# An attention and routing kernel whose engines take their work in the order of the source, with the routed work laid out anew

## The chip, the cores and the metric

The program runs on one core of a Trainium2 chip. The core has a matrix engine (TensorE, PE in the rows; its weight loads are listed apart as PEld), a vector engine (VectorE, DVE), an activation engine (ScalarE, ACT), GpSimd (POOL) and a queue engine that issues transfers (SyncE, SP). Each runs its own list of instructions in order, and semaphores tie the lists together. The metric is the device time of the core in microseconds (us), the median of three runs.

## What is computed

All inputs and outputs are float32.

```python
batch, n_heads, seq, head_dim = (8, 12, 448, 64)
...
scores = scale * np.matmul(q, k.transpose(0, 1, 3, 2)) - np.log(S)
attn = 1.0 / (1.0 + np.exp(-scores))
return np.matmul(attn, v)
...
# bridge: (B,H,S,D) -> (B, S, H*D), D = 768
scores = np.einsum('bsd,d->bs', x, w_gate)
out = x.copy()
for b in range(B):
    top_idx = np.argpartition(-scores[b], capacity)[:capacity]   # capacity 128
    xe = x[b, top_idx]
    h = np.maximum(xe @ w1, 0.0)            # w1: 768 x 1024
    ye = h @ w2                             # w2: 1024 x 768
    g = 1.0 / (1.0 + np.exp(-scores[b, top_idx]))
    out[b, top_idx] = x[b, top_idx] + g[:, None] * ye
```

So each of the 8 images (batch entries) goes through sigmoid attention, and then the 128 of its 448 tokens with the highest gate score go through two dense layers. All others are copied.

## The kernel before

**Attention steps.** The kernel walks through 24 steps `i`, three for each image, each with four heads. `load(i)` has SyncE issue 16 transfers (k, q and two pieces of v). `turn(i)` transposes k and q on VectorE into `kT` and `qT`. `scores(i, n)`, n from 0 to 6, multiplies them on TensorE into a score tile `psc` in PSUM (two buffers), and ScalarE takes its sigmoid into `attnT`; a third group of scores must therefore wait until the sigmoid of the first has read its tile. `values(i)` multiplies `attnT` with v into two tiles `pav`; its first matmuls (line 194) read the last sigmoid's result. VectorE copies `pav` into `xT`. `back(i, pr)`, twice for each step, turns 448 columns of `xT` back with four transposes on TensorE into the PSUM tile `ps`, and VectorE copies that into the image's `x_b`.

**Routed work of an image**, once its `x_b` is whole: `store_and_gate` has SyncE store `x_b` twice (to the output and to a scratch tensor `x_d`) and computes the gate scores on VectorE (four reductions) and a `diag` tile on GpSimd. `rank` has one wide and one small matmul (lines 247, 249), then eight comparisons with sums on VectorE (line 259) and the selection matrix `sel` (line 265). `select` multiplies `sel` with the token numbers (line 274) and has GpSimd gather the chosen rows `xe` from `x_d`. `turn_rows`, two halves, transposes `xe` (line 294). `ffn1` is 8 pieces of six matmuls, with a Relu on ScalarE after each four pieces; `ffn2` is two parts of eight matmuls, each ended by a VectorE instruction into `oe`. `scatter` has GpSimd write `oe` to the output.

**Buffers that bind these together.** `back`, `rank`, `select` and `turn_rows` share one PSUM tile (pool `ps_1`, one buffer; the names `ps_...` in the order rows are its successive uses). `ffn1` and `ffn2` share another (`psf`). `x_b`, `oe`, `sel`, `attnT` and `hT` have one buffer each, so the first copy into the next image's `x_b` must wait until both stores of this image have read it.

**What sets the order.** Each step has two half-steps; a table `places` says which functions belong to half-step `s`, `back` first and the routed work after it. `fill(2*i)` runs between score groups 3 and 4 of step `i`, `fill(2*i + 1)` between group 6 and `values(i)`. That is the order of the source. The framework's scheduler then orders the instructions of each engine anew by priorities and by its own estimates of when inputs are ready, so what an engine runs is not what the source says:

```python
for i in range(NI):
    for n in range(NF + 1):
        scores(i, n)
    if i == 0:
        load_weights()
    fill(2 * i)
...
```

Of the kernel before, what the change touches and what calls it, by code (L numbers as in the profile page):

```python
# [9 lines left out]
F32 = mybir.dt.float32  # L10
# [6 lines left out]
def kernel(  # L17
# [17 lines left out]
    P = 128  # L35
# [3 lines left out]
    NF = 3  # L39
# [4 lines left out]
    KF = F // P  # L44
    ND = D // 2
    NI = B * NQ
# [18 lines left out]
    ps_f = ctx.enter_context(tc.tile_pool(name="ps_f", bufs=1, space=PSUM))  # L65
# [5 lines left out]
    def load(i):  # L71
        b, g = divmod(i, NQ)
        h0 = 4 * g
        tiles = []
        for nm, src in (("k", k), ("q", q)):

            t = raw.tile([P, 2, TB * Dh], F32, name=f"raw_{nm}")
            for j in range(2):
                for e in range(2):
                    p0 = (2 * j + e) * TT  # L80
                    nc.sync.dma_start(  # L81
                        out=t[p0:p0 + TT, :, 0:RUN],
                        in_=bass.AP(
                            tensor=src.tensor,
                            offset=src.offset + (b * H + h0 + j) * S * Dh + e * TT,
                            ap=[[TB * Dh, TT], [2 * S * Dh, 2], [1, RUN]]),
                    )
            tiles.append(t)

        tv = vals.tile([P, 4, NF * Dh], F32, name="raw_v")  # L90
        for m in range(4):
            nc.sync.dma_start(
                out=tv[m * TT:(m + 1) * TT],
                in_=bass.AP(tensor=v.tensor,
                            offset=v.offset + (b * H + h0) * S * Dh + NF * m * Dh,
                            ap=[[TB * Dh, TT], [S * Dh, 4], [1, NF * Dh]]))

        th = vals.tile([P, 2, Dh], F32, name="raw_h")
        for pr in range(2):
            for m in range(2):  # L100
                p0 = (2 * pr + m) * TT
                nc.sync.dma_start(
                    out=th[p0:p0 + TT],
                    in_=bass.AP(tensor=v.tensor,
                                offset=(v.offset + (b * H + h0 + 2 * pr) * S * Dh
                                        + (4 * NF + m) * Dh),
                                ap=[[TB * Dh, TT], [S * Dh, 2], [1, Dh]]))
        raws[i] = tiles + [tv, th]
# [20 lines left out]
    def late_consts():  # L129
        nc.gpsimd.dma_start(  # L130
            out=wg_b,
            in_=bass.AP(tensor=moe_w_gate.tensor, offset=moe_w_gate.offset,
                        ap=[[0, CP]] + [list(x) for x in moe_w_gate.ap]),
        )
        nc.gpsimd.memset(ones, 1.0)
        nc.gpsimd.memset(ones_row, 1.0)
        nc.gpsimd.iota(iota_r, pattern=[[1, CAP]], base=0, channel_multiplier=0,
                       allow_small_or_imprecise_dtypes=True)
        for t in tok_gate:
            nc.gpsimd.iota(t[:, :, 0], pattern=[[CP, NCH]], base=0,  # L140
                           channel_multiplier=1, allow_small_or_imprecise_dtypes=True)
        nc.gpsimd.memset(earlier, 0.0)
        for c in range(NCH):
            nc.gpsimd.affine_select(
                out=earlier[:, c, :], in_=earlier[:, c, :], compare_op=ALU.is_ge,
                fill=1.0, base=-c * CP, pattern=[[1, S]], channel_multiplier=-1)

    def load_weights():
        for w, src in ((w1_sb, moe_w1), (w2_sb, moe_w2)):
            nc.gpsimd.dma_start(out=w, in_=src.rearrange("(t p) f -> p t f", p=P))  # L150
# [4 lines left out]
    def turn(i):  # L155


        kT[i] = head.tile([P, 2, TB, TT], F32, name="kT")
        src = raws[i][0].rearrange("p a (r d) -> p a r d", d=Dh)
        for pr in range(2):  # L160
            nc.vector.transpose(  # L161
                kT[i][:, pr, :4 * NF],
                src[:, pr, :4 * NF, 0:TT].rearrange("p (m c) d -> p c m d", c=NF))
        nc.vector.transpose(kT[i][:, :, 4 * NF:], src[:, :, 4 * NF:, 0:TT])
        qT[i] = head.tile([P, 2, TB, TT], F32, name="qT")
        src = raws[i][1].rearrange("p a (r d) -> p a r d", d=Dh)
        nc.vector.transpose(qT[i], src[:, :, :, 0:TT])  # L167

    def scores(i, n):

        if n == 0:
            attn[i] = attnp.tile([P, 2 * NF + 1, 2, S], F32, name="attnT")
        psc = ps_sc.tile([P, 2, 512], F32, name="psc")
        parts = [(pr, slice(4 * NF, TB), pr * Dh, Dh) for pr in range(2)]
        if n < 2 * NF:
            parts = [(n // NF, slice(4 * (n % NF), 4 * (n % NF) + 4), 0, P)]
        for pr, rows, p0, np_ in parts:
            for j in range(2):
                d = slice(j * Dh, (j + 1) * Dh)
                nc.tensor.matmul(  # L180
                    psc[p0:p0 + np_, j, :S],
                    kT[i][d, pr, rows, :].rearrange("e r t -> e (r t)"),
                    qT[i][d, pr].rearrange("e r t -> e (r t)"),
                    start=True, stop=True)
        nc.scalar.activation(attn[i][:, n], psc[:, :, :S], AF.Sigmoid,  # L185
                             bias=bias_s, scale=QK_SCALE)
# [37 lines left out]
    st = {}  # L224
# [83 lines left out]
        if f % 4 == 3:  # L308
            nc.scalar.activation(st[b]["hT"][:, f - 3:f + 1, :n], ps[:, :, :n], AF.Relu)  # L309

    def ffn2(b, n, part):
        hT = st[b]["hT"]
        if part == 0:
            st[b]["oe"] = moe.tile([P, D], F32, name="oe")
        oe = st[b]["oe"]
        ps = ps_f.tile([P, 512], F32, name="psf")
        cols = slice(part * ND, (part + 1) * ND)
        for t in range(KF):
            nc.tensor.matmul(ps[:n, :ND], hT[:, t, :n], w2_sb[:, t, cols],  # L319
                             start=(t == 0), stop=(t == KF - 1))  # L320
        nc.vector.scalar_tensor_tensor(  # L321
            out=oe[:n, cols], in0=ps[:n, :ND], scalar=st[b]["gate"][:n, 0:1],
            in1=st[b]["xe"][:n, cols], op0=ALU.mult, op1=ALU.add)
# [5 lines left out]
            in_=st[b]["oe"][:n], in_offset=None)  # L329


    places = {}

    def put(s, fn, *args):
        places.setdefault(s, []).append((fn, args))

    def routed(b):
        s = 2 * NQ * (b + 1) + 1
        put(s, store_and_gate, b)
        put(s + 2, rank, b)  # L340
        s += 4
        for s0, n in SLOTS:
            put(s, select, b, s0, n)
            for half in range(2):
                put(s + 1 + half, turn_rows, b, n, half)
            for f in range(KF):
                put(s + 2 + f // 2, ffn1, b, n, f)
            for part in range(2):
                put(s + 2 + KF // 2 + part, ffn2, b, n, part)
            put(s + 2 + KF // 2 + 1, scatter, b, n)  # L350
            s += 2 + KF // 2 + 2

    for i in range(NI):
        put(2 * i + 2, back, i, 0)
        put(2 * i + 3, back, i, 1)
    fills = {s: list(v) for s, v in places.items()}
    places = {}
    for b in range(B):
        routed(b)
    order = {}  # L360
    last = max(places)
    for s in range(last + 1):
        own, rest = fills.get(s, []), places.get(s, [])
        order[s] = own + rest

    def fill(s):
        for fn, args in order.get(s, []):
            fn(*args)

    turn(0)  # L370
    late_consts()
    for i in range(NI):
        for n in range(NF + 1):
            scores(i, n)
        if i == 0:
            load_weights()
        fill(2 * i)
        for n in range(NF + 1, 2 * NF + 1):
            scores(i, n)
        if i + 1 < NI:  # L380
            turn(i + 1)
        if i + 2 < NI:
            load(i + 2)
        fill(2 * i + 1)
        values(i)
    for s in range(2 * NI, last + 1):
        fill(s)


# [27 lines left out]
```

## Time and profile before

| | |
|---|---|
| Time, median of 3 runs | 755.27 us (750.07 to 758.37) |
| The profiled execution's own time | 751.88 us |
| Its span, first to last instruction | 750.1 us |
| TensorE busy with matmuls | 571.5 us (76%) |
| VectorE, ScalarE, GpSimd busy | 229.3, 174.0, 31.2 us |
| Mean granted TensorE clock | 0.899 of full speed |
| DMA, mean over the span | 119 GB/s |

Busy times are sums over the span and say nothing of where an engine stood idle. Each float32 matmul of the program appears as two records in the trace, so a count there is twice that of the order's rows. In the rows, a bracket gives the idle time of the engine just before the first instruction of the row, and who ended it. The difference between time and span, 1.78 us, lies outside the recorded instructions.

### The profile page before, as it was taken

What the parts mean: (1) busy time and instruction counts of PE and PEld (TensorE: products, weight loads), DVE (VectorE), ACT (ScalarE), POOL (GpSimd) and SP (SyncE); (2) the same over time, 40 slices, a digit from 0 to 9 for tenths busy, and PEclk for the clock granted to TensorE, in tenths of its full rate; (3) what the DMA queues carried; (4) which work ended last, traced back from release to release, by engine and by line L of the source; (5) the groups of instructions that cost most, each with busy time, mean ns of one, the idle gap of its engine ahead of it and who ended that gap; (6) DMA issues with size and microseconds to landing.
All of it is one profiled execution on the core that took longest, in us unless ns stands there. A gap on an engine that the chain in (4) does not pass through costs nothing.

```text
span 750.1 us, 7353 instructions
## 1 busy us (share of the span) xinstructions
PE 571.5 (76%) x2896; PEld 295.0 (39%) x2896; DVE 229.3 (31%) x481; ACT 174.0 (23%) x193; POOL 31.2 (4%) x43
## 2 busy tenths in 40 slices
PE   0767678679983889839896599856998388984996
PEld 0222222346332554324542454324633245423873
DVE  1032421642115312254034521164121641225410
ACT  0333243031330322303412033302133033130000
POOL 4000000000000000000000000001000000000010
PEclk9889899869997799959999699987999689995999
DMA  9989595258132673227550392505923251002310
GB/s 247 305 191 207 120 262 124 47 128 237 43 94 69 164 175 77 63 68 205 134 140 1 78 267 64 140 22 116 265 53 94 68 156 64 1 21 61 109 43 21
DMA packets 46995, 88.93 MB, mean 119 GB/s; under 512 B 12848, under 2 KB 25136, under 8 KB 46960
## 3 DMA queue, kind: packets, MB, share of 16 engines
q1 hardware_dynamic: 44288, 75.52, 41.0%
q0 software_dynamic: 2672, 12.93, 5.4%
q8 instruction: 23, 0.38, 0.2%
q14 instruction: 12, 0.10, 0.0%
HBM read 63.26 MB, written 25.17 MB: 118 GB/s over the span
## 4 chain that ended last, share of the span: by engine, by line
PE 58%; DMA 13%; ACT 11%; DVE 10%; issue 6%; SPq 2%; POOLq 0%; DVEq 0%; ACTq 0%
PE pav L200 14%; PE psf L306 12%; PE psc L180 12%; PE psf L319 10%; ACT attnT L185 10%; DMA raw_q<-in_q_dram 5%; DMA xe<-x_d,row 4%; DVE junk L259 3%; PE ps L219 3%; PE pav L194 3%; DMA raw_h<-in_v_dram 2%; PE ps L274 2%; SPq L81 2%; PE ps L294 1%; DVE x_b L221 1%
## 5 line engine op out<-in xcount | busy, mean ns | idle before, releaser
L185 ACT ACTIVATE attnT<-psc,bias_s 128x896 f32<-128x896 f32 x168 | 161.8, 1004 | 292.3 <-PE psc L180 292.0
L180 PE MATMUL psc<-qT,kT 64*128 64x448 f32 (+1 forms) x768 | 165.6, 597 | 48.3 <-DVE qT L167 29.8
L200 PE MATMUL pav<-attnT,raw_v 128*64 128x448 f32 x576 | 124.5, 551 | 0.0
L205 DVE COPY xT<-pav 128x448 f32<-128x448 f32 x48 | 44.2, 923 | 243.1 <-PE pav L200 243.1
L180 PEld LDWEIGHTS psc<-qT,kT 64*128 64x128 f32 (+1 forms) x768 | 53.5, 180 | 151.1 <-ACT attnT L185 101.3
L306 PE MATMUL psf<-xeT,w_sb 128*128 128x128 f32 x768 | 104.6, 297 | 9.4 <-ACT hT L309 4.9
L306 PEld LDWEIGHTS psf<-xeT,w_sb 128*128 128x128 f32 x768 | 99.0, 210 | 18.6 <-DVE xeT L296 7.5
L319 PE MATMUL psf<-w_sb,hT 128*128 128x384 f32 x256 | 90.1, 497 | 10.9 <-ACT hT L309 5.5
L200 PEld LDWEIGHTS pav<-attnT,raw_v 128*64 128x64 f32 x576 | 40.3, 138 | 72.5 <-issue 69.6
L319 PEld LDWEIGHTS psf<-w_sb,hT 128*128 128x128 f32 x256 | 46.3, 189 | 51.7 <-DVE oe L321 9.7
L221 DVE COPY x_b<-ps 112x512 f32<-112x512 f32 x48 | 33.0, 688 | 106.5 <-PE ps L219 105.6
L219 PE MATMUL ps<-iden,xT 128*112 128x128 f32 x192 | 37.8, 329 | 22.7 <-DVE x_b L221 12.0
L274 PE MATMUL ps<-tok_gate,sel 112*128 112x2 f32 x64 | 13.8, 338 | 43.0 <-DVE sel L265 43.0
L219 PEld LDWEIGHTS ps<-iden,xT 128*112 128x112 f32 x192 | 23.5, 154 | 45.9 <-issue 14.8
L194 PE MATMUL pav<-attnT,raw_h 64*64 64x448 f32 x192 | 26.4, 568 | 15.9 <-ACT attnT L185 13.5
L309 ACT ACTIVATE hT<-psf 128x512 f32<-128x512 f32 x16 | 9.6, 597 | 122.6 <-PE psf L306 122.6
L161 DVE STREAM_TRANSPOSE kT<-raw_k 128x384 f32<-128x384 f32 x48 | 25.2, 553 | 34.7 <-DMA raw_k<-in_k_dram 34.7
L281 ACT ACTIVATE gate<-ps 128x1 f32<-128x1 f32 x8 | 1.4, 171 | 143.0 <-DVE idx L279 143.0
L321 DVE SCALAR_TENSOR_TENSOR oe<-psf,gate,xe 128x384 f32<-128x384 f32 x16 | 9.9, 618 | 72.0 <-PE psf L319 70.6
L274 PEld LDWEIGHTS ps<-tok_gate,sel 112*128 112x128 f32 x64 | 13.5, 311 | 45.3 <-issue 45.0
L234 DVE CUSTOM_DVE_ANT_0 junk<-x_b,wg_b 112x768 f32<-112x768 f32 x32 | 30.3, 948 | 1.3
L294 PE MATMUL ps<-iden,xe 128*128 128x128 f32 x48 | 13.1, 407 | 22.9 <-DMA xe<-x_d,row 22.0
(38 smaller groups left out, 171.7 us busy)
## 6 DMA issues: line engine op xcount, KB each, us to landing
raw_k<-in_k_dram SPq DMA_DIRECT2D x96, 216.0 KB, 4.4
raw_q<-in_q_dram SPq DMA_DIRECT2D x96, 216.0 KB, 4.9
out_dram<-x_b SPq DMA_DIRECT2D x8, 1344.0 KB, 6.4
x_d<-x_b SPq DMA_DIRECT2D x8, 1344.0 KB, 11.3
raw_v<-in_v_dram SPq DMA_DIRECT2D x96, 96.0 KB, 4.8
w_sb<-in_moe_w_dram POOLq DMA_DIRECT2D x2, 3072.0 KB, 24.4
raw_h<-in_v_dram SPq DMA_DIRECT2D x96, 16.0 KB, 3.4
wg_b<-in_moe_w_gate_dram POOLq DMA_DIRECT2D x1, 336.0 KB, 8.3
```

The lines of the kernel that those rows point to most:

```text
L161: nc.vector.transpose(kT[i][:, pr, :4 * NF], src[:, pr, :4 * NF, 0:TT].rearrange("p (m c) d -> p c m d", c=NF))
L180: nc.tensor.matmul(psc[p0:p0 + np_, j, :S], kT[i][d, pr, rows, :].rearrange("e r t -> e (r t)"), qT[i][d, pr].rearrange("e r t -> e (r t)" ...
L185: nc.scalar.activation(attn[i][:, n], psc[:, :, :S], AF.Sigmoid, bias=bias_s, scale=QK_SCALE)
L194: nc.tensor.matmul(out_t[pr][j * Dh:(j + 1) * Dh], th[p, j, :], attn[i][p, 2 * NF, j, :], start=True, stop=False)
L200: nc.tensor.matmul(out_t[pr][j * Dh:(j + 1) * Dh], tv[:, 2 * pr + j, c * Dh:(c + 1) * Dh], attn[i][:, pr * NF + c, j, :], start=False, sto ...
L205: nc.vector.tensor_copy(xT[i][:, pr].rearrange("p (t r) -> p r t", r=TB), out_t[pr].rearrange("p (r t) -> p r t", t=TT))
L219: nc.tensor.transpose(ps[:CP, c, :], xT[i][:, pr, c * CP:(c + 1) * CP], iden)
L221: nc.vector.tensor_copy(x_tiles[b][:, :, hp * P:(hp + 1) * P], ps[:CP])
L234: nc.vector.tensor_tensor_reduce(out=junk, in0=x_b[:, c, :], in1=wg_b, scale=1.0, scalar=0.0, op0=ALU.mult, op1=ALU.add, accum_out=tg[:, c ...
L274: nc.tensor.matmul(pk[:n, 0:2], sel[:, c, s0:s0 + n], tg[:, c, :], start=(c == 0), stop=(c == NCH - 1))
L306: nc.tensor.matmul(ps[:, f % 4, :n], w1_sb[:, t, f * P:(f + 1) * P], xeT[:, t, :n], start=(t == 0), stop=(t == KD - 1))
L319: nc.tensor.matmul(ps[:n, :ND], hT[:, t, :n], w2_sb[:, t, cols], start=(t == 0), stop=(t == KF - 1))
```

## The change

The whole emission runs under the framework's manual schedule, in which each engine issues its instructions in the order of the source. The table of places is split in two: `short` holds `back`, `store_and_gate`, `rank`, `select` and `turn_rows` (all but `store_and_gate` use the shared PSUM tile), `long` holds `ffn1`, `ffn2` and `scatter`. `fill` goes through the short pieces and puts a share of the long ones behind each. `ffn2`'s parts are cut into pairs of matmuls so that they can be shared out. Both halves of `turn_rows` now stand in one half-step, the one before `ffn1` begins (the second half shared a half-step with the first pieces of `ffn1` before). `load(i + 2)` is written at the head of step `i`, and `load_weights()` at the head of step 1 instead of in step 0.

```diff
-    def ffn2(b, n, part):
+    def ffn2(b, n, part, t0):
...
-        for t in range(KF):
+        for t in range(t0, t0 + 2):
...
+        if t0 + 2 < KF:
+            return
...
+    short, long = {}, {}
...
         s = 2 * NQ * (b + 1) + 1
-        put(s, store_and_gate, b)
-        put(s + 2, rank, b)
+        put(short, s, store_and_gate, b)
+        put(short, s + 2, rank, b)
         s += 4
         for s0, n in SLOTS:
-            put(s, select, b, s0, n)
+            put(short, s, select, b, s0, n)
             for half in range(2):
-                put(s + 1 + half, turn_rows, b, n, half)
+                put(short, s + 1, turn_rows, b, n, half)
             for f in range(KF):
-                put(s + 2 + f // 2, ffn1, b, n, f)
+                put(long, s + 2 + f // 2, ffn1, b, n, f)
+            s += 2 + KF // 2
             for part in range(2):
-                put(s + 2 + KF // 2 + part, ffn2, b, n, part)
-            put(s + 2 + KF // 2 + 1, scatter, b, n)
-            s += 2 + KF // 2 + 2
+                for t0 in range(0, KF, 2):
+                    put(long, s + part, ffn2, b, n, part, t0)
+            put(long, s + 1, scatter, b, n)
+            s += 2
...
     def fill(s):
-        for fn, args in order.get(s, []):
+        a, z = short.get(s, []), long.get(s, [])
+        done = 0
+        for n, (fn, args) in enumerate(a):
             fn(*args)
...
+            upto = (n + 1) * len(z) // len(a)
+            for f, x in z[done:upto]:
+                f(*x)
+            done = upto
+        for f, x in z[done:]:
+            f(*x)
+
+    def stream():
+        turn(0)
+        late_consts()
+        for i in range(NI):
+            if i + 2 < NI:
+                load(i + 2)
+            if i == 1:
+                load_weights()
...
+    with tc.manual_schedule():
+        stream()
```

**From `rank` to `select` on TensorE**, in the middle of the program. Before, the end of an image's third step and what follows it (`ps_...` are uses of the shared PSUM tile):

```order
L219 MATMUL ps_1784<-iden,xT 112x128 x4
L200 MATMUL pav<-attnT,raw_v 64x448 x4
L247 MATMUL ps_1803<-diag,ones 112x448
L249 MATMUL ps_1803<-tok_gate_142,iden 112x4
L200 MATMUL pav<-attnT,raw_v 64x448
L219 MATMUL ps_1870<-iden,xT 112x128 x4
L219 MATMUL ps_1929<-iden,xT 112x128 x4
L274 MATMUL ps_1946<-tok_gate_142,sel 128x2 x4
```

Now, from the ranking matmuls of one image to its selection:

```order
L249 MATMUL ps_1799<-tok_gate_142,iden 112x4
L306 MATMUL psf<-xeT,w_sb 128x128 x6
L194 MATMUL pav<-attnT,raw_h 64x448 x4
L200 MATMUL pav<-attnT,raw_v 64x448 x12
L180 MATMUL psc<-qT,kT 128x448 x8
L219 MATMUL ps_1892<-iden,xT 112x128 x4
L306 MATMUL psf<-xeT,w_sb 128x128 x12
L180 MATMUL psc<-qT,kT 128x448 x4
L180 MATMUL psc<-qT,kT 64x448 x4
L219 MATMUL ps_1931<-iden,xT 112x128 x4
L320 MATMUL psf<-w_sb,hT 128x384 x4
L274 MATMUL ps_1943<-tok_gate_142,sel 128x2 x4
```

Two groups of transposes and one matmul stood between ranking and selecting; now a `values`, seven score groups and two `back`s and 22 matmuls of the dense layers of the image before stand there.

**From the gather to the dense layers on TensorE.** Before, right behind the selection (`xe` is the gathered tile):

```order
L219 MATMUL ps_1997<-iden,xT 112x128 x4
L294 MATMUL ps_2015<-iden,xe 128x128 x3
L219 MATMUL ps_2060<-iden,xT 112x128 x4
L306 MATMUL psf<-xeT,w_sb 128x128 x3
L294 MATMUL ps_2066<-iden,xe 128x128 x3
L306 MATMUL psf<-xeT,w_sb 128x128 x9
```

Now, right behind the selection:

```order
L320 MATMUL psf<-w_sb,hT 128x384 x4
L194 MATMUL pav<-attnT,raw_h 64x448 x4
L200 MATMUL pav<-attnT,raw_v 64x448 x12
L180 MATMUL psc<-qT,kT 128x448 x8
L219 MATMUL ps_2019<-iden,xT 112x128 x4
L320 MATMUL psf<-w_sb,hT 128x384 x2
L294 MATMUL ps_2029<-iden,xe 128x128 x3
L320 MATMUL psf<-w_sb,hT 128x384 x4
L294 MATMUL ps_2038<-iden,xe 128x128 x3
L320 MATMUL psf<-w_sb,hT 128x384 x2
```

The first transposition of gathered rows stood behind one group of transposes; now half a part of `ffn2`, a `values`, four score groups, one `back` and two more matmuls stand between, and the two halves are parted by four matmuls.

**On VectorE, where a new image's `x_b` is begun** (rows with what each waits for; DMAHW entries are transfers). Before:

```order
L321 SCALAR_TENSOR_TENSOR oe<-psf,gate,xe 128x384 [waits PE_49]
L221 COPY x_b<-ps_1313 112x4x128 [waits DMAHW5_49,DMAHW4_49,DVE_49]
L221 COPY x_b<-ps_1372 112x4x128 [waits PE_49]
L205 COPY xT<-pav 128x14x32 [waits DVE_49]
L252 COPY rep<-ps_1391 112x452 [waits PE_49]
```

Now:

```order
L205 COPY xT<-pav 128x14x32 [waits PE_49] x2
L221 COPY x_b<-ps_1335 112x4x128 [waits DMAHW4_49,DMAHW5_49,DVE_49,PE_49]
L161 STREAM_TRANSPOSE kT<-raw_k 128x384 [waits DMAHW7_49,DMAHW6_49]
L161 STREAM_TRANSPOSE kT<-raw_k 128x384
L164 STREAM_TRANSPOSE kT<-raw_k 128x2x64
L167 STREAM_TRANSPOSE qT<-raw_q 128x896 [waits DMAHW2_49,DMAHW3_49,DMAHW1_49,DMAHW0_49]
L221 COPY x_b<-ps_1374 112x4x128 [waits PE_49]
L252 COPY rep<-ps_1387 112x452 [waits PE_49]
```

The copy that waits for the two stores stood behind the end of the dense layers; now the next step's transposes of k and q are queued behind it.

On SyncE the order of the transfers is the same before and after. On GpSimd the first weight transfer, which stood ahead of the four instructions that fill `earlier` (line 144), now stands behind them; the second stood behind them already.

## Rows read from the trace of the kernel before

**Rows 1.** Busy time of each engine in three stages, granted clock, DMA share

```profile
core 0: us, PE busy (x) PEld busy (x) DVE busy (x) ACT busy (x) POOL busy (x), PEclk, DMA share, GB/s
44.39:161.52 117.13, 85.17 (x402) 35.75 (x402) 41.63 (x83) 34.17 (x36) 2.09 (x3) 0.87 0.64 149
161.52:672.44 510.92, 411.07 (x2119) 209.24 (x2118) 154.21 (x318) 128.98 (x143) 16.49 (x17) 0.91 0.43 109
672.44:750.10 77.66, 56.40 (x305) 43.73 (x304) 25.86 (x68) 2.73 (x6) 4.86 (x5) 0.86 0.17 56
```

**Rows 2.** TensorE in order of time, one image: start, duration, idle before

```profile
504.40 1.84 PE L274 MATMUL ps<-tok_gate,sel 112*128 112x2 f32 x8 [6.39 <-DVE sel L265]
506.82 1.10 PE L219 MATMUL ps<-iden,xT 128*112 128x128 f32 x4 [0.58 <-ACT gate L281]
511.14 0.87 PE L294 MATMUL ps<-iden,xe 128*128 128x128 f32 x3 [3.22 <-DMA xe<-x_d,row]
...
535.69 5.62 PE L306 MATMUL psf<-xeT,w_sb 128*128 128x128 f32 x48 [0.69 <-ACT hT L309]
...
542.85 1.77 PE L180 MATMUL psc<-qT,kT 64*128 64x448 f32 x8
545.04 1.92 PE L180 MATMUL psc<-qT,kT 64*128 64x448 f32 x8 [0.42 <-ACT attnT L185]
...
549.30 0.98 PE L180 MATMUL psc<-qT,kT 64*64 64x448 f32 x8 [0.21 <-ACT attnT L185]
...
551.70 0.98 PE L194 MATMUL pav<-attnT,raw_h 64*64 64x448 f32 x8
552.61 4.73 PE L200 MATMUL pav<-attnT,raw_v 128*64 128x448 f32 x24
...
561.53 5.43 PE L319 MATMUL psf<-w_sb,hT 128*128 128x384 f32 x16 [0.77 <-DVE oe L321]
...
575.45 1.08 PE L194 MATMUL pav<-attnT,raw_h 64*64 64x448 f32 x8 [1.13 <-ACT attnT L185]
...
579.61 0.65 PE L219 MATMUL ps<-iden,xT 128*112 128x128 f32 x4
...
581.84 1.01 PE L247 MATMUL ps<-diag,ones 112*112 112x448 f32 x2
...
585.98 0.65 PE L219 MATMUL ps<-iden,xT 128*112 128x128 f32 x4 [1.55 <-DVE x_b L221]
593.01 1.84 PE L274 MATMUL ps<-tok_gate,sel 112*128 112x2 f32 x8 [6.38 <-DVE sel L265]
```

**Rows 3.** Two stretches of that image, columns as in rows 1

```profile
504.40:515.00 10.60, 6.15 (x26) 5.28 (x27) 2.97 (x9) 0.17 (x1) 0.97 (x1) 0.50 0.50 121
...
545.00:555.00 10.00, 9.54 (x50) 3.29 (x52) 0.00 (x0) 5.70 (x6) 0.00 (x0) 1.00 0.01 3
```

**Rows 4.** VectorE, ranking without other work between, first and last row

```profile
703.44 0.63 DVE L252 COPY rep<-ps 112x452 f32<-112x452 f32 x1 [8.13 <-PE ps L249]
...
710.14 0.88 DVE L265 TENSOR_SCALAR sel<-iota_r,above 112x128 f32<-112x128 f32 x4
```

**Rows 5.** Transfers: gather (median us to landing), store to `x_d`, SyncE behind it

```profile
xe<-x_d,row POOLq DMA_INDIRECT x8, 4.3
...
DMA to landing us min/median/max: 10.0/11.3/11.7
...
525.85 8.01 SPq L81 DMA_DIRECT2D raw_k<-in_k_dram  x4
```

**Rows 6.** GpSimd: the four instructions that now precede the first weights

```profile
5.78 2.11 POOL L144 TENSOR_SCALAR_AFFINE_SELECT earlier<-earlier 112x448 f32<-112x448 f32 x4
```

**Rows 7.** TensorE at the start of step 1

```profile
44.39 5.49 PE L180 MATMUL psc<-qT,kT 64*128 64x448 f32 x16 [1.80 <-DVE qT L167]
```

**Rows 8.** The tail: selection and turning between dense layers, and the end

```profile
712.14 0.95 PE L274 MATMUL ps<-tok_gate,sel 112*128 112x2 f32 x8
...
718.33 0.49 PE L294 MATMUL ps<-iden,xe 128*128 128x128 f32 x3
...
744.54 0.62 DVE L321 SCALAR_TENSOR_TENSOR oe<-psf,gate,xe 128x384 f32<-128x384 f32 x1 [5.52 <-PE psf L319]
```

More of the change, by code (lines that the diff above doesn't have):

```diff
@@ L309, in ffn1 @@
             nc.scalar.activation(st[b]["hT"][:, f - 3:f + 1, :n], ps[:, :, :n], AF.Relu)
-    def ffn2(b, n, part):
+    def ffn2(b, n, part, t0):
         hT = st[b]["hT"]
-        if part == 0:
+        if part == 0 and t0 == 0:
             st[b]["oe"] = moe.tile([P, D], F32, name="oe")
-        oe = st[b]["oe"]
-        ps = ps_f.tile([P, 512], F32, name="psf")
+        if t0 == 0:
+            st[b]["psf"] = ps_f.tile([P, 512], F32, name="psf")
+        oe, ps = st[b]["oe"], st[b]["psf"]
         cols = slice(part * ND, (part + 1) * ND)
-        for t in range(KF):
+        for t in range(t0, t0 + 2):
             nc.tensor.matmul(ps[:n, :ND], hT[:, t, :n], w2_sb[:, t, cols],
                              start=(t == 0), stop=(t == KF - 1))
+        if t0 + 2 < KF:
+            return
         nc.vector.scalar_tensor_tensor(
@@ L329, in scatter, with put @@
             in_=st[b]["oe"][:n], in_offset=None)
-    places = {}
-    def put(s, fn, *args):
-        places.setdefault(s, []).append((fn, args))
+    short, long = {}, {}
+    def put(where, s, fn, *args):
+        where.setdefault(s, []).append((fn, args))
     def routed(b):
         s = 2 * NQ * (b + 1) + 1
-        put(s, store_and_gate, b)
-        put(s + 2, rank, b)
+        put(short, s, store_and_gate, b)
+        put(short, s + 2, rank, b)
         s += 4
         for s0, n in SLOTS:
-            put(s, select, b, s0, n)
+            put(short, s, select, b, s0, n)
@@ L353 @@
+            put(long, s + 1, scatter, b, n)
+            s += 2
     for i in range(NI):
[L354 to L357, printed above, removed]
+        for pr in range(2):
+            put(short, 2 * i + 2 + pr, back, i, pr)
     for b in range(B):
         routed(b)
[L360 to L364, printed above, removed]
+    last = max(max(short), max(long))
@@ L366, in fill @@
     def fill(s):
-        for fn, args in order.get(s, []):
+        a, z = short.get(s, []), long.get(s, [])
+        done = 0
+        for n, (fn, args) in enumerate(a):
             fn(*args)
[L370 to L385, printed above, removed]
@@ L386 @@
-    for s in range(2 * NI, last + 1):
-        fill(s)
+            upto = (n + 1) * len(z) // len(a)
[12 more added lines that the diff above has]
+                load_weights()
+            for n in range(NF + 1):
+                scores(i, n)
+            fill(2 * i)
+            for n in range(NF + 1, 2 * NF + 1):
+                scores(i, n)
+            if i + 1 < NI:
+                turn(i + 1)
+            fill(2 * i + 1)
+            values(i)
+        for s in range(2 * NI, last + 1):
+            fill(s)
```

## The prediction

> **What bounds the kernel now.** I read the stages first, then one image on TensorE in order of time, then the engines that end its waits. In the long middle stage TensorE is busy 411.1 of 510.9 us, while VectorE has 154.2 and ScalarE 129.0 and the DMA engines are busy 0.43 of it [rows 1]. TensorE is the bound, but stands idle a fifth of the time, and its granted clock is 0.91 there. The image in order of time shows where. From one selection (504.40) to the next (593.01) are 88.6 us. In it TensorE waits 6.4 us for the ranking on VectorE, 3.2 us for the gathered rows, 1.55 us for a copy out of the shared PSUM tile, and 0.6 to 0.8 us at a time behind single copies, Relus and dense-layer ends [rows 2]. Between score groups it waits 0.42 or 0.21 us for ScalarE, and 1.13 us before `values` where nothing is put in between. Each long wait also costs clock: the stretch that begins behind the 6.4 us wait has a granted clock of 0.50, that is 1.2 GHz, where the later stretch with waits of only 0.2 to 0.4 us has 1.00, or 2.4 GHz [rows 3]. The selection takes 1.84 us there, and 0.95 us in the tail between dense matmuls [rows 2, 8].
>
> **The change, part by part.** The sum is made against the profiled execution (span 750.1, own time 751.88, which is 3.4 us under the median of the three runs).
>
> *The long waits.* Ranking takes VectorE 7.6 us from its first copy to the end of `sel` [rows 4]. Between ranking and selecting TensorE now has a `values`, seven score groups, two `back`s and 22 dense matmuls, over 20 us by the prices below. The wait of 6.4 us goes. The gather lands 4.3 us after its issue [rows 5]; with index and issue I call that 6 us, and half a part of `ffn2` (2.7), a `values` (5.6), four score groups (4.1), a `back` and two matmuls lie over it. That wait goes too. Nothing on VectorE is late next: its 154.2 us over these 18 steps [rows 1] are 8.6 a step, under a step's time of some 22.
>
> *The short waits.* Behind each `back` or turned half there are now two or more dense matmuls (1.4 us) or scores, against a copy of 0.7 us. The waits for Relu and for `oe` (0.69, 0.77) fall behind three score groups. They cost nothing while there is dense work to share out; without that cover each would cost 0.6 to 0.8 us again, which is so in steps 4 and 5 and in the tail.
>
> *Prices per image at full clock* [rows 2, 8]. Score groups 0 to 3: from 542.85 to 546.96, 4.11 us with their waits. Groups 4 to 6, which start on free tiles because the fill ahead has let ScalarE catch up: 1.77 + 0.42 + 0.98 = 3.17. `values`: 551.70 to 557.34, 5.64. Three steps: 38.8. Six `back`s of 0.65: 3.9. `ffn1`: two times 5.62, 11.2. `ffn2`: two times 5.43, 10.9. Ranking 1.0, selecting 0.95, turning two times 0.49. Sum 67.8 us, where the trace has 88.6.
>
> *Transposes between matmuls.* Four transposes of a `back` take 0.65 us among matmuls and 1.10 us behind the long wait [rows 2]; I price all at 0.65. The Trainium skill (TensorE: Matmul & The Clock Gate, Part 4) says that transposes don't engage the full clock, because they don't count as busy work; by that, `back`s set singly into half-steps could run at the slow price, and 48 of them would add 21.6 us to my sum. The row at 579.61 stands between matmuls and has the fast price, so I leave it out.
>
> *Start.* SyncE's order is the same. The first weights now stand behind 2.11 us of GpSimd work [rows 6] and have no other wait, so "later" is about 2 us of a transfer that is needed a hundred us later. Its bytes still compete with the first loads. I leave the start of step 1 at 44.4 us [rows 7]; the bounds are a loss of 2 and a gain of 2 us (the 1.80 us wait that ends there stands behind copies on VectorE that now come later).
>
> *Steps 1 to 5,* which lack dense work. Step 1 starts at the slow clock: its first 16 records take 5.49 [rows 7], then 0.65 + 3.17 + 0.65, 0.48 (the rest of the 1.13 behind a `back`) and 5.64, together 16.1. Steps 2 and 3: 14.7 each. Step 4 adds the ranking and the new wait: VectorE's first copy into the next `x_b` waits for both stores, and queued behind it are the transposes for the next step and the copy that frees the shared PSUM tile. The store to `x_d` lands up to 11.7 us after issue [rows 5]; without dense work only 10.4 us lie between the last copy of one image and the first of the next (5.64 + 4.11 + 0.65), and SyncE may still be issuing a load. I take 4 us for it (bounds 0 and 9): 19.2. Step 5: 14.7 less 0.48, plus 0.85 for the shared tile and 0.95 for selecting, 16.0. That makes 80.7, and step 6 starts at 125.1, where the trace has 161.5.
>
> *Steps 6 to 23.* Here 2.8 us of `ffn1` are added, so the stores have 13.2 us, and if they are late TensorE has another 6 us (`ffn1` and three score groups) before it needs what is queued: cost nothing. Six images of 67.8, less one part of `ffn2` (5.4), plus 1.5 in step 6 for a shared tile without cover: 402.9, against 510.9 [rows 1].
>
> *Tail.* After the last `values` come two `back`s 1.3, five parts of `ffn2` (one of the sixth image, two each of the last two) 27.2, two `ffn1` 22.5, turning 2.0, ranking 1.0, 2 us of waiting for ranking (7.6 under half an `ffn1`, 5.6), selecting 0.95, and four short waits of 0.7: 59.8. From the last VectorE instruction to the end are 5.6 [rows 8]. Together 65.4, against 77.7.
>
> *Sum.* 125.1 + 402.9 + 65.4 = 593.4, and 1.8 outside it: 595. I add an allowance of 7 us for hand-overs that I priced at nothing (0 to 3 us per image; I take the value nearest to a single short wait of 0.8), and 3 us to come to the median of runs: **605 us**, 20% less than now.
>
> **Rivals.** *The stores as the new wait (640 us).* With images 21 us shorter the same bytes move faster: the DMA share of 0.43 becomes about 0.56. SyncE takes 8 us to issue one k load right behind the stores [rows 5], so they do share the engines. If the pair takes twice as long, 23 us, VectorE is held 10 us in each image (23 less 13.2), 6 of them covered, and seven images lose 4 to 5 us each, 35 in all. Against it: 11.7 is the longest of eight, with a load beside it each time.
>
> *Only the routed waits go (about 650 us).* The scores keep their present price if ScalarE's queue, now with a Relu or gate between sigmoids, starts late: 8.56 us (542.85 to 550.28, and the 1.13 [rows 2]) instead of 7.28 for seven groups, 24 times, and the short waits return at half their cost, some 2 us an image. That is 31 and 14 more. Against it: ScalarE is busy a quarter of the stage, and a Relu stands in the half-step where ScalarE is idle.
>
> *The clock falls (slower than before).* The short PSUM pieces leave TensorE a small wait in every half-step, and if those waits alone brought the slow clock, everything but the ScalarE-bound scores would take twice its price: per image 67.8 less 21.8 of scores is 46, so 46 us more, and 18 steps would give 276 more, 881 us. It decides from the point where a little over half of the half-steps run slow (150 us lost). Against it: the granted clock is 1.00 over stretches with such waits every few us [rows 3], and even the 1.55 us wait is followed by a `back` at 0.65. The Trainium skill (TensorE: Matmul & The Clock Gate, A second HAM failure mode) describes this: cycling through PSUM banks with micro-idles between groups makes the clock swing. By that rule this change, which adds such pieces, would fall on the slow side; the trace disagrees with it for waits of 0.2 to 0.8 us.
>
> *The change does less than it says.* The weights hardly move, as said; were they truly out of the way at the start, the first loads would land sooner and step 1 would start before 44.4. At best that gives the wait of TensorE there and a few us of loads, some 5 us: 600. No wait in the program holds the weights back, so I count this inside the forecast's own case.
>
> **How the numbers follow.** The forecast 605 has a chance of 0.75, the stores 0.08, the partial gain 0.07, transposes at the slow price (627) 0.04, the clock 0.04, and no change to speak of 0.02. The low end is the sum without allowance, with the start 2 us earlier and the store wait at nothing: 588. The high end takes in the stores and the partial gain: 650. Faster by over 1% (about what a measurement of this kernel can tell) 0.94, within 1% 0.02, slower 0.04.
>
> **What would show it.** Right: on TensorE the rows at the selection carry no wait for `sel`, those at the turning none for `xe`, the selection takes about 0.95 us, and the granted clock is 0.98 or more from step 6 to the tail; three steps take 68 to 70 us; step 4 has a wait on VectorE ended by a transfer. Wrong: a wait of VectorE for the stores or raw loads in every image, waits of scores for `qT`, or a granted clock below 0.9 without long waits. The forecast falls if handing over between engines costs more than 3 us per image.

## The result, and the profile after

The changed kernel takes **582.4 us**, the median of four runs (581.8 to 583.4). The kernel before had 754.1 us in four runs beside it. The ratio is 0.772, with a 95% interval of 0.768 to 0.777, so the time fell by 23%. The forecast was 605 us with a range of 588 to 650: the direction and the mechanism were right, and the time lies 5.6 us below the low end.

The profiled run took 583.43 us, 581.7 of them in the span. The stages are cut at the same points of the work as in [rows 1], with the start ahead of them; columns as there.

```profile
core 0: us, PE busy (x) PEld busy (x) DVE busy (x) ACT busy (x) POOL busy (x), PEclk, DMA share, GB/s
15.60:44.07 28.47, 13.74 (x65) 4.68 (x65) 2.49 (x5) 6.76 (x7) 0.00 (x0) 0.85 0.96 274
44.07:127.28 83.21, 72.40 (x373) 27.93 (x373) 38.18 (x73) 33.94 (x36) 1.99 (x2) 0.93 0.94 215
127.28:515.27 387.99, 373.03 (x2158) 197.74 (x2157) 174.18 (x355) 129.41 (x144) 16.59 (x17) 1.00 0.56 143
515.27:581.70 66.43, 55.27 (x306) 40.97 (x304) 18.57 (x44) 2.56 (x5) 4.92 (x5) 0.95 0.19 66
```

Most of the gain, 122.9 of the 168.4 us of span, lies in the middle stage, which fell from 510.9 [rows 1] to 388.0 us. Its clock rose from 0.91 to 1.00. The sum of busy TensorE time fell too, from 411.1 to 373.0 us, although the stage holds a few more records than before (2158 and 2119): matmuls no longer run at 1.2 GHz behind long waits. The other stages fell by 33.9 us (steps 1 to 5) and 11.2 us (the tail). The new place of the line that loads the weights gave nothing at the start: step 1 begins at 44.07 us, before at 44.39 [rows 7].

Here is one image of the changed kernel on TensorE in order of time (start, duration, idle time before it and what ended that), which answers to [rows 2]:

```profile
385.24 1.77 PE L180 MATMUL psc<-qT,kT 64*128 64x448 f32 x8
387.43 1.92 PE L180 MATMUL psc<-qT,kT 64*128 64x448 f32 x8 [0.41 <-ACT attnT L185]
389.28 0.65 PE L219 MATMUL ps<-iden,xT 128*112 128x128 f32 x4
389.77 1.46 PE L320 MATMUL psf<-w_sb,hT 128*128 128x384 f32 x4
391.06 0.49 PE L294 MATMUL ps<-iden,xe 128*128 128x128 f32 x3
391.39 2.75 PE L320 MATMUL psf<-w_sb,hT 128*128 128x384 f32 x8
...
397.82 0.98 PE L180 MATMUL psc<-qT,kT 64*64 64x448 f32 x8 [0.36 <-ACT attnT L185]
...
401.99 0.98 PE L194 MATMUL pav<-attnT,raw_h 64*64 64x448 f32 x8
402.90 4.73 PE L200 MATMUL pav<-attnT,raw_v 128*64 128x448 f32 x24
407.56 1.77 PE L180 MATMUL psc<-qT,kT 64*128 64x448 f32 x8
...
419.73 0.92 PE L247 MATMUL ps<-diag,ones 112*112 112x448 f32 x2
...
441.11 0.95 PE L274 MATMUL ps<-tok_gate,sel 112*128 112x2 f32 x8
441.93 2.83 PE L320 MATMUL psf<-w_sb,hT 128*128 128x384 f32 x8
...
450.25 1.77 PE L180 MATMUL psc<-qT,kT 64*128 64x448 f32 x8
```

From 385.24 to 450.25 are 65.0 us, against 88.6 [rows 2]. The waits for `sel`, for `xe` and behind the `back`s are gone; what is left are the waits of score groups for ScalarE, 0.35 to 0.42 us. The ranking (419.73) stands 21 us ahead of the selection (441.11). The second thing to see is that many rows start before the row ahead of them ends by its duration: the `back` at 389.28 lasts 0.65 us, and the next matmuls start 0.49 us after it did. That is where the forecast's sum went wrong (below).

In step 4 the new wait on the store is there, as forecast. First VectorE, then TensorE in the same step; the last row of TensorE is from step 5:

```profile
99.59 0.69 DVE L221 COPY x_b<-ps 112x512 f32<-112x512 f32 x1 [9.18 <-DMA x_d<-x_b]
```

```profile
100.34 1.09 PE L219 MATMUL ps<-iden,xT 128*112 128x128 f32 x4 [3.23 <-DVE x_b L221]
103.13 1.80 PE L247 MATMUL ps<-diag,ones 112*112 112x448 f32 x2 [1.71 <-DVE x_b L221]
...
105.06 1.77 PE L194 MATMUL pav<-attnT,raw_h 64*64 64x448 f32 x8
...
120.72 1.05 PE L274 MATMUL ps<-tok_gate,sel 112*128 112x2 f32 x8 [0.78 <-DVE x_b L221]
```

VectorE is held 9.18 us. TensorE waits 3.23 us for the copy that was held and 1.71 us for the next copy, which stands on VectorE behind the transposes of k and q. What follows runs at the slow price for a while: the `back` takes 1.09 instead of 0.65 us, the first part of `values` 1.77 instead of 0.98.

### The profile page after: what moved, and what is told of

It reads as the page before. It is cut to its first block, busy times and chain, and to the rows that moved or that the text cites. A ratio compares the mean times of both kernels' runs of the same rounds, so it can differ in the third digit from the quotient of the medians.

```text
span 581.7 us, 7332 instructions
## 1 busy us (share of the span) xinstructions
PE 514.4 (88%) x2896; PEld 271.3 (47%) x2896; DVE 235.8 (41%) x481; ACT 174.0 (30%) x193; POOL 31.3 (5%) x43
## 4 chain that ended last, share of the span: by engine, by line
PE 71%; DMA 9%; ACT 8%; issue 6%; DVE 4%; SPq 0%; POOLq 0%; POOL 0%; ACTq 0%; DVEq 0%
PE psc L180 19%; PE pav L200 18%; PE psf L320 12%; PE psf L306 11%; ACT attnT L185 8%; DMA raw_q<-in_q_dram 5%; PE ps L219 4%; PE pav L194 4%; DMA raw_h<-in_v_dram 2%; DMA x_d<-x_b 2%; DVE junk L234 1%; PE ps L247 1%; PE ps L274 1%; DVE junk L259 1%; PE ps L294 1%
## 5 line engine op out<-in xcount | busy, mean ns | idle before, releaser
L180 PE MATMUL psc<-qT,kT 64*128 64x448 f32 (+1 forms) x768 | 160.0, 584 | 46.2 <-DVE qT L167 28.7
L200 PE MATMUL pav<-attnT,raw_v 128*64 128x448 f32 x576 | 113.7, 544 | 0.0
L306 PE MATMUL psf<-xeT,w_sb 128*128 128x128 f32 x768 | 92.2, 276 | 1.7 <-DVE oe L324 1.0
L306 PEld LDWEIGHTS psf<-xeT,w_sb 128*128 128x128 f32 x768 | 88.4, 192 | 2.8 <-DVE oe L324 1.8
L219 PEld LDWEIGHTS ps<-iden,xT 128*112 128x112 f32 x192 | 19.8, 134 | 35.6 <-issue 25.8
L219 PE MATMUL ps<-iden,xT 128*112 128x128 f32 x192 | 31.5, 287 | 3.2 <-DVE x_b L221 3.2
L167 DVE STREAM_TRANSPOSE qT<-raw_q 128x896 f32<-128x896 f32 x24 | 25.8, 1075 | 10.5 <-DMA raw_h<-in_v_dram 6.4
L259 DVE SCALAR_TENSOR_TENSOR junk<-rep,earlier 112x448 f32<-112x448 f32 x32 | 21.9, 685 | 1.4
L259 DVE SCALAR_TENSOR_TENSOR junk<-rep,ones_row 112x448 f32<-112x448 f32 x32 | 21.9, 685 | 1.2
L283 POOL DMA_INDIRECT xe<-x_d,row x8 | 8.0, 1006 | 266.8 <-DVE idx L279 229.5
```

What stands on the lines that cost most here:

```text
L180: nc.tensor.matmul(psc[p0:p0 + np_, j, :S], kT[i][d, pr, rows, :].rearrange("e r t -> e (r t)"), qT[i][d, pr].rearrange("e r t -> e (r t)" ...
L200: nc.tensor.matmul(out_t[pr][j * Dh:(j + 1) * Dh], tv[:, 2 * pr + j, c * Dh:(c + 1) * Dh], attn[i][:, pr * NF + c, j, :], start=False, sto ...
L219: nc.tensor.transpose(ps[:CP, c, :], xT[i][:, pr, c * CP:(c + 1) * CP], iden)
L259: nc.vector.scalar_tensor_tensor(out=junk, in0=rep[:, :S], scalar=rep[:, S + c:S + c + 1], in1=mask, op0=cmp, op1=ALU.mult, accum_out=cnt[ ...
L306: nc.tensor.matmul(ps[:, f % 4, :n], w1_sb[:, t, f * P:(f + 1) * P], xeT[:, t, :n], start=(t == 0), stop=(t == KD - 1))
```

## The experiments

All eight do the whole work of the reference. The kernel before ran beside each (medians 754.5 and 755.0 us, and 754.1 beside the changed kernel); the changed kernel did not, so differences from it of a few us are taken between series, and the traces are read beside them. The first two take the order and the places apart.

**The order alone, in the places of before.** The kernel before, with its own last loop written under the manual order.

```diff
-    turn(0)
-    late_consts()
-    for i in range(NI):
...
+    with tc.manual_schedule():
+        turn(0)
+        late_consts()
+        for i in range(NI):
...
```

> The kernel before with nothing but the manual schedule: its own table of places, load order and weight order, each engine in source order. Theory (the order alone removes the long waits, and the source of before already puts dense work of the image before ahead of ranking and selecting): 580 to 590 us, three steps in about 65 us. Rival (the new places and the sharing out carry a good part): 600 to 640 us, with waits of 0.6 to 0.8 us at the shared PSUM tile or 3 us at the gather.

Measured: 588.9 us, 0.781 of before (0.777 to 0.786). An image takes 66.04 us (388.64 to 454.68), 1.03 us more than in the changed kernel. Over six images that is 6.2 us; the medians differ by 6.4, and the two profiled executions (588.34 and 583.43) by 4.9. One wait makes most of it: routed turning stands straight behind a `back`, whose copy must first free the shared PSUM tile.

```profile
403.23 0.55 PE L294 MATMUL ps<-iden,xe 128*128 128x128 f32 x3 [0.79 <-DVE x_b L221]
```

So the order by itself gives about 165 of the 172 us, and the rest of the edit (above all the new places for short and long pieces) some 6.

**The places alone, in the scheduler's order.** The changed kernel without the manual order.

```diff
-    with tc.manual_schedule():
-        stream()
+    stream()
```

> The changed kernel without the manual schedule: new places, cut dense layers, earlier loads, but the scheduler orders each engine. Theory (the order is what matters): the scheduler pulls selection and turning forward again and the 6.4 and 3.2 us waits come back, 700 to 760 us. Rival (the places matter as much): 620 to 680 us.

Measured: 753.9 us, 0.999 (0.996 to 1.002), no change. Two groups of TensorE's instructions (line, tile, count, busy time and mean, then the idle time before them and what ended it) show why. First this kernel, then the changed one:

```profile
L274 PE MATMUL ps<-tok_gate,sel 112*128 112x2 f32 x64 | 13.8, 338 | 43.8 <-DVE sel L265 43.8
L294 PE MATMUL ps<-iden,xe 128*128 128x128 f32 x48 | 13.4, 415 | 27.3 <-DMA xe<-x_d,row 22.7 <-DVE xeT L296 4.6
```

```profile
L294 PE MATMUL ps<-iden,xe 128*128 128x128 f32 x48 | 8.0, 275 | 1.4 <-DVE x_b L221 0.8 <-DVE xeT L296 0.6
L274 PE MATMUL ps<-tok_gate,sel 112*128 112x2 f32 x64 | 7.9, 245 | 2.5 <-DVE sel L265 1.7 <-DVE x_b L221 0.8
```

Without the manual order TensorE waits 43.8 us for `sel` in eight selections and 27.3 us at the turning, although the source puts other work between. With it, 2.5 and 1.4 us. Here the source's places were worth nothing where the order wasn't kept.

**Selecting early.** The changed kernel with the selection moved to the half-step of its own ranking, so that no other half-step lies between.

```diff
-            put(short, s, select, b, s0, n)
+            put(short, s - 2, select, b, s0, n)
```

> The changed kernel with select in the half-step of rank, so that only six dense matmuls stand between. Theory (the early selection was the largest single loss of the kernel before, as wait and as clock): TensorE waits 6.2 us for sel in each image and then runs at the slow clock through the selection, half an ffn1 piece and part of values, 9 to 10 us an image in all, 650 to 660 us. Rival (the wait alone counts, the clock does not fall): 6.2 to 7 us an image, 625 to 635 us.

Measured: 659.8 us, 0.875 (0.870 to 0.879), 77 us more than the changed kernel. An image takes 75.17 us (382.09 to 457.26), 10.2 more. On TensorE in order of time, and then the granted clock behind the wait:

```profile
402.20 1.84 PE L274 MATMUL ps<-tok_gate,sel 112*128 112x2 f32 x8 [5.72 <-DVE sel L265]
403.90 2.91 PE L306 MATMUL psf<-xeT,w_sb 128*128 128x128 f32 x12
406.74 1.77 PE L194 MATMUL pav<-attnT,raw_h 64*64 64x448 f32 x8
```

```profile
402.20:413.20 11.00, 11.00 (x52) 6.32 (x52) 1.60 (x6) 0.17 (x1) 0.99 (x1) 0.70 0.24 58
```

The wait of 5.72 us is under 60% of the price. Behind it TensorE is busy without a gap for 11 us, yet at a granted clock of 0.70: the twelve records of `ffn1` (six matmuls) take 2.91 us, in the changed kernel 1.50 to 1.58, and the first part of `values` 1.77, where the changed kernel has 0.98 for the latter. This is the cost of a long wait that [rows 2] and [rows 3] showed, made again by one edit. The stretch of six images is 60.6 us longer than in the changed kernel; the rest of the 77 lies in steps 4 and 5 (a wait of 7.51 us for `sel`) and in the tail.

**All short pieces first, then the long ones.** The changed kernel without the lines that share the long pieces out.

```diff
             fn(*args)
-            upto = (n + 1) * len(z) // len(a)
-            for f, x in z[done:upto]:
-                f(*x)
-            done = upto
         for f, x in z[done:]:
```

> The changed kernel with all short pieces of a half-step ahead of its long ones. Theory (sharing out only hides the single copies out of the shared PSUM tile): per image four bare waits, 0.65 to 0.85 us each, as steps 5 and 6 of the changed kernel show them (0.78, 0.78, 0.65): 3.0 us an image in the middle stage, 18 to 21 us in all, 601 us. Rival (the weight-load queue or the copies hide them anyway): 583 to 587 us.

Measured: 612.1 us, 0.812 (0.807 to 0.816), 29.7 us more than the changed kernel, where some 19 were expected. An image takes 69.03 us (379.69 to 448.72), 4.0 more. Four waits are new in it:

```profile
391.47 1.05 PE L274 MATMUL ps<-tok_gate,sel 112*128 112x2 f32 x8 [0.79 <-DVE x_b L221]
...
408.77 0.55 PE L294 MATMUL ps<-iden,xe 128*128 128x128 f32 x3 [0.78 <-DVE x_b L221]
409.97 0.55 PE L294 MATMUL ps<-iden,xe 128*128 128x128 f32 x3 [0.65 <-DVE xeT L296]
...
439.35 0.98 PE L247 MATMUL ps<-diag,ones 112*112 112x448 f32 x2 [0.87 <-DVE x_b L221]
```

They sum to 3.1 us. The missing 0.9 us are overlaps that a wait takes away, about a quarter of a microsecond at each. Five images at 4.0 make 20 us. The first of the six has only 0.9 more, since the changed kernel has two of the waits there too. One image has another 3.4 us: the same selection, behind the same wait of 0.79 us, is followed there by a slow clock (rows in the last section). That is 24.4 us for the middle stage. The steps before it have 1.7 more, most of it in a `values` at the slow clock in step 5, and the stage behind 541.35 (68.85 us, against 66.43 from the same point in the changed kernel) 2.4. Together these are the 28.5 us between the two profiled executions. The direction held and the size did not: the forecast had the waits, but neither the lost overlap, as in the prediction's own sum, nor the clock.

**Two buffers for `x_b`,** so that the copies of the next image needn't wait for the stores of the last.

```diff
-            x_tiles[b] = moe.tile([CP, NCH, D], F32, name="x_b")
+            x_tiles[b] = moe.tile([CP, NCH, D], F32, name="x_b", bufs=2)
```

> The changed kernel with two buffers for x_b, so that no copy waits for the stores. Theory (the store wait costs TensorE only in step 4: 3.23 and 1.71 us and the slow clock behind them, some 2 us): 575 to 577 us, middle stage unchanged at 65 us an image. Rival (the store wait also holds VectorE in every image): 560 us or less. Second rival (what follows on SyncE is late instead): 581 to 583 us.

Measured: 576.2 us, 0.765 (0.761 to 0.769), 6.2 us less than the changed kernel. The waits of 3.23 and 1.71 us in step 4 are gone, and what is left there is one behind the shared PSUM tile:

```profile
98.11 0.98 PE L247 MATMUL ps<-diag,ones 112*112 112x448 f32 x2 [0.88 <-DVE x_b L221]
```

So the store wait cost some 6.2 us: 4.9 of waiting on TensorE, less the 0.88 that shows instead, and the slow clock behind it. In the traces, from the `values` of step 3 to that of step 5, it is 6.5 us (38.0 in the changed kernel, 31.5 here).

**The weights truly later.** The changed kernel with the weights on SyncE's queue, one behind the loads of step 1 and one behind those of step 4.

```diff
-    def load_weights():
-        for w, src in ((w1_sb, moe_w1), (w2_sb, moe_w2)):
-            nc.gpsimd.dma_start(out=w, in_=src.rearrange("(t p) f -> p t f", p=P))
+    def load_weights(n):
+        w, src = ((w1_sb, moe_w1), (w2_sb, moe_w2))[n]
+        nc.sync.dma_start(out=w, in_=src.rearrange("(t p) f -> p t f", p=P))
...
-            if i == 1:
-                load_weights()
+            if i in (1, 4):
+                load_weights(i // 4)
```

> The changed kernel with the two weight transfers on SyncE's queue, behind load(3) and load(6), instead of on GpSimd at 7 us. Theory (in the changed kernel the weights' bytes still hold the first loads back, since the edit moves them by 2 us only): step 1 starts near 31 us instead of 44.1, at the full clock, 566 to 570 us. Rival (what is saved is given back in steps 2 to 6, where the DMA engines are 0.94 busy): 575 to 582 us. Second rival (the first loads are held by their own queue): step 1 after 40 us, 580 us.

Measured: 574.4 us, 0.761 (0.756 to 0.765), between the theory and its first rival. On TensorE in order of time, then on VectorE:

```profile
31.01 1.77 PE L180 MATMUL psc<-qT,kT 64*128 64x448 f32 x8
...
91.38 1.10 PE L219 MATMUL ps<-iden,xT 128*112 128x128 f32 x4 [9.03 <-DVE x_b L221]
94.17 1.81 PE L247 MATMUL ps<-diag,ones 112*112 112x448 f32 x2 [1.69 <-DVE x_b L221]
```

```profile
90.63 0.69 DVE L221 COPY x_b<-ps 112x512 f32<-112x512 f32 x1 [14.97 <-DMA x_d<-x_b]
```

Step 1 starts 13.1 us earlier and at the full price (1.77 for the first eight score records). Some of it is given back in step 4, where the wait on the store grows from 9.18 to 14.97 us on VectorE and from 3.23 to 9.03 on TensorE, 5.8 us more. The store itself lands as before (10.4 to 11.5 us, and 10.4 to 11.9 in the changed kernel). It is issued late: `x_b` is whole at 69.12, and the store is issued 9.9 us after that, in the changed kernel 4.2 us (83.88 and 88.05). VectorE stands from 75.66, while SyncE's queue is still at a load.

```profile
75.35 3.12 SPq L102 DMA_DIRECT2D raw_h<-in_v_dram  x4
...
79.02 0.46 SPq L230 DMA_DIRECT2D x_d<-x_b  x1
```

**Both together,** the last two edits at once.

> Two buffers for x_b and the late weights together. Theory (the two gains lie in different places, the store wait in step 4 and the loads in step 0): 6 us under the run with the late weights alone, 560 to 564 us. Rival (both free the same stretch up to step 6, which the DMA engines then bound): no more than 2 us under the better of the two.

Measured: **562.6 us**, 0.748 (0.743 to 0.752), 19.8 us or 3.4% less than the changed kernel, and the fastest of all. The edits alone gave 6.2 and 8.0 us. Together they give 5.6 more than that sum, since the second buffer also takes away the wait that the earlier start had made longer. The theory's number was met by luck: it counted 6 us under the late weights, which came out some 6 us above their own forecast, and the gain on them is 11.8. Stages cut as above, save that the last cut lies 1.1 us earlier in the work, and one stretch within them:

```profile
31.40:108.31 76.91, 69.56 (x375) 26.47 (x373) 37.82 (x72) 33.80 (x36) 1.99 (x2) 0.98 0.94 249
101.90:108.30 6.40, 6.40 (x28) 2.05 (x24) 0.92 (x1) 0.00 (x0) 0.74 (x1) 0.73 1.03 410
108.31:494.00 385.69, 370.37 (x2154) 197.03 (x2154) 174.33 (x355) 129.30 (x144) 16.60 (x17) 1.00 0.62 154
```

Steps 1 to 5 take 76.9 us instead of 83.2, and step 6 begins at 108.3 instead of 127.3. The middle stage is as it was but for 1.2 us in step 6 (386.8 us by the cut used above, and 388.0), with the DMA share at 0.62.

**Every `back` twice,** to measure the price of a transpose between matmuls: each group transposes its four chunks two times into the same tile.

```diff
-        for c in range(NCH):
+        for c in list(range(NCH)) * 2:
```

> The changed kernel with every transpose of back done twice into the same place (four more in each of 48 groups, same result). Theory (a group's price on TensorE is the distance from its start to the next group's, 0.49 us, not the duration of its row): 48 x 0.49 = 23 us more, some of it under bare waits in steps 1 to 5: 603 to 606 us. Rival (the row's duration, 0.65, as the prediction priced it): 31 us, 612 to 615 us. Second rival (transposes bring the slow clock, 1.10 each group): 53 us or more, 635 us.

Measured: 599.7 us, 0.795 (0.791 to 0.799), 17.3 us more than the changed kernel. One group and its follower:

```profile
401.03 1.08 PE L219 MATMUL ps<-iden,xT 128*112 128x128 f32 x8
401.95 1.46 PE L320 MATMUL psf<-w_sb,hT 128*128 128x384 f32 x4
```

A transpose is one record in the trace, where the other matmuls have two. A doubled group takes 0.92 us from its start to the next start, the single one 0.49 (389.28 to 389.77), so four more transposes cost 0.43 us: 17.3 us are 40 such groups. Both prices that were offered are too high (0.49 and 0.65), and the theory of the smaller one is the nearer. The difference of the durations, 1.08 less 0.65, gives the same 0.43: the error in a duration is its end, once for each row. The mean granted clock of the run is 0.980, against 0.974 in the changed kernel. The Trainium skill (TensorE: Matmul & The Clock Gate, Part 4: PE-mode transpose) says that the full clock doesn't engage for transposes; by that, the added ones would run at the price of 1.10 us for four, and the trace shows 0.43.

## Why the prediction was right in kind and 23 us too high

**The part that failed is "Prices per image at full clock",** which summed to 67.8 us where 65.0 were measured. The pieces and the waits in it were all there. But it added the durations of rows, and a row's duration reaches past the start of the next row: matmuls are pipelined, and the page of the profile warns that their ends are modelled. From start to start the same pieces are shorter, in the image shown above:

- a `back` ahead of dense matmuls 0.49 us (389.28 to 389.77), forecast 0.65; six of them make 1.0
- turning 0.33 (391.06 to 391.39), forecast 0.49; two make 0.3
- score groups 0 to 3 4.04 (385.24 to 389.28), forecast 4.11, and `values` 5.57 (401.99 to 407.56), forecast 5.64
- the selection 0.82 (441.11 to 441.93), forecast 0.95.

It could have been seen beforehand: [rows 2] has `values` begin at 551.70 with a row of 0.98, and its next row at 552.61, not 552.68. A tenth here and there on some forty rows is 2.8 us an image, 14 us over the five images that are alike. The first of the six was forecast at 63.9 and took 62.9: its two bare waits, 0.78 and 0.65 us, were in the forecast with 1.5 us, but the overlap lost at them and 1.2 us of slow clock behind them were not, and they pay back most of what the shorter prices save. With the prices went the sign that three steps take 68 to 70 us.

**The allowance of 7 us for hand-overs** had the wrong sign for the same cause. A hand-over between TensorE's rows costs nothing where no wait stands between; it overlaps by 0.07 to 0.16 us in the rows above. The 3 us to come to the median of runs weren't there either (the median lies 1.0 us under the profiled run).

Term by term, from 605 down to 582.4: steps 6 to 23 −14.9 (402.9 forecast, 388.0 measured), steps 1 to 5 +2.5 (80.7 and 83.2; step 4 alone +3.1, 19.2 and 22.3), the tail +1.0 (65.4 and 66.4), the start −0.3, the allowance −7, the median −4.0; rounding makes the rest. The low end 588 took off the allowance, the start and the store wait (which gives 589, and 592 with the 3 us to the median), but left the prices as they were: no bound stood on the largest term.

**The long waits** went as forecast. `sel` and `xe` hold TensorE nowhere in the middle stage; early selection brought back 77 us, and the scheduler's order all 171.5.

**The short waits** cost nothing where dense work is shared out, and 0.65 to 0.87 us each where it isn't (short pieces first). The forecast's figure of 0.6 to 0.8 misses the lost overlap of about a quarter of a microsecond.

**Transposes between matmuls** were priced at the fast row, and that was the right choice of the two.

**The start** was right: 44.4 and 44.07. The line for the weights stands later, but their queue on GpSimd has nothing to wait for. Their issue begins at 7.05 us in the kernel with the order alone and at 7.07 in the changed one. Put behind loads on SyncE's queue, they give step 1 back 13.1 us, more than the 5 that the forecast called the best case.

**Step 4** has its wait on VectorE ended by a transfer. It was priced at 4 us, TensorE's own waits are 4.9, and two buffers gain 6.2 with the clock. From step 6 on the store costs nothing visible, as forecast.

**The rivals.** Stores as the new wait in every image: no, VectorE waits for a store only twice, 9.18 us in step 4 and 3.92 us at 412.52, where TensorE has no gap, and for loads only up to step 1, although the DMA share of the stage became 0.56 as that rival had it. Only the routed waits go: no, score groups wait 0.35 to 0.42 us; the forecast had 0.42. The clock falls: no, it is 1.00 over 388 us in which TensorE has such a wait every few us. The Trainium skill (TensorE: Matmul & The Clock Gate, A second HAM failure mode) tells of a swinging clock behind micro-idles between groups; waits of this size don't show it here. The prediction said the same of waits up to 0.8 us, but the stretch of 1.00 in [rows 3] has only waits of 0.42 and 0.21 us, and behind 0.65 to 0.79 us the clock did fall at some places, the changed kernel's step 6 among them (last section).

## What to carry to other kernels

Price a stretch of an in-order engine by the distance from start to start, not by the sum of durations, and where a wait is added, price the lost overlap beside the wait. Where an engine waits for another engine's result, other work in the source helps only if the order that runs is the order written: here the places alone gave nothing, the order alone 165 us, both 172. A transfer is moved by what its queue must wait for, not by the line where it stands; and when one wait is taken away, look at what the earlier start will meet, since two edits that gave 6 and 8 us gave 20 together.

## What the runs showed of the hardware that was not expected

The clock can fall behind short waits, and the wait alone doesn't decide it. In the tail of the changed kernel, and then in the kernel with both edits, the same selection has the same wait:

```profile
536.52 1.13 PE L274 MATMUL ps<-tok_gate,sel 112*128 112x2 f32 x8 [1.70 <-DVE sel L265]
537.51 6.98 PE L320 MATMUL psf<-w_sb,hT 128*128 128x384 f32 x16
```

```profile
516.34 1.02 PE L274 MATMUL ps<-tok_gate,sel 112*128 112x2 f32 x8 [1.70 <-DVE sel L265]
517.22 5.41 PE L320 MATMUL psf<-w_sb,hT 128*128 128x384 f32 x16
```

In the one the sixteen records (eight matmuls) take 6.98 us, in the other 5.41. The granted clock of the first stretch is 0.77, a mean between the levels of 1.2 and 2.4 GHz. And in the kernel with both edits the stretch from 101.90 to 108.30 (its row stands above) has 0.73, behind a wait of only 0.97 us. Shorter waits do it too. The kernel with all short pieces first has such a selection in every image. Here are the rows of one image, and then a row of a later one:

```profile
319.07 1.36 PE L274 MATMUL ps<-tok_gate,sel 112*128 112x2 f32 x8 [0.79 <-DVE x_b L221]
320.29 8.47 PE L320 MATMUL psf<-w_sb,hT 128*128 128x384 f32 x16
...
392.38 5.41 PE L320 MATMUL psf<-w_sb,hT 128*128 128x384 f32 x16
```

The last row stands behind the selection at 391.47 (its row stands above), with the same wait of 0.79 us. From 320.50 to 325.50 the granted clock is 0.50. In the changed kernel a stretch of step 6 is like it, with 0.74 from 134.00 to 140.50:

```profile
133.94 0.55 PE L294 MATMUL ps<-iden,xe 128*128 128x128 f32 x3 [0.65 <-DVE xeT L296]
134.42 4.32 PE L180 MATMUL psc<-qT,kT 64*128 64x448 f32 x16
```

What decides stays open: no run here tells it apart. In these traces such a stretch costs 1.2 to 3.4 us, so a difference of that size between two profiled executions can be the clock alone.
